# An S4 convolution and MLP mixer on one core: the spectra scratch laid out by frequency row, and a new order of the work

## The chip, the cores and the metric

The kernel runs on one core of one Trainium2 chip. The metric is device time in microseconds (us) of one execution; three executions of the kernel before took 552.21 to 555.27 us, with a median of 553.7. One more was profiled.

## The reference

All of it works on sequences of L = 2048 steps of D = 512 channels in float32. What matters here is the convolution, which is computed through spectra:

```python
xn = _layernorm(x, axis=-1)
# s = A(xn): a convolution over time, one filter per channel
P = jnp.exp(logdA[:, :, None] * l[None, None, :])
K = jnp.einsum("dn,dnl,dn->dl", Cc, P, dB).real          # (512, 2048)
Kf = rfft(pad(K, 2L));  Uf = rfft(pad(u.T, 2L))
y = irfft(Uf * Kf)[..., :L].T + u * Dskip
# g = silu(B(xn)): token shifts and an MLP
h = _gelu(_layernorm(x, axis=-1) @ w1)                    # 512 -> 512
x1 = x + concat(h's four quarters shifted by +1, -1, +2, -2) @ w2
x1 + _gelu(_layernorm(x1, axis=-1) @ w3) @ w4             # 512 -> 1376 -> 512
# the whole
return x + s * g
```

## The kernel before

**Tiling.** Time step t*16 + s lies in partition t of slice s of `X` [128, 16, 512], so the whole sequence stays in SBUF. The channels are worked on in two halves of DH = 256. A transform of the sequence is split in two steps over 64 rows of frequency ("g") with real and imaginary part ("e"), so 128 rows in all, and 16 slices with two parities ("s", "r").

**Stages.** `token_mixing` computes the layer norm, the first step of the input's transform (`u_stage1`, which stores `ue` to the DRAM scratch `scr_Ud`), and the shifted mixing. `tables` builds the filter in 16 chunks of 32 channels on ACT (exponentials, sines) and DVE (multiplies of the tile `wv`), sums over the states on PE, takes the first transform step of the filter on PE, and stores `k1e` to `scr_Kfa` (chunks 0 to 7) or `scr_Kfb` (8 to 15). `products` runs in 8 steps for each half: load `uin` and `kin` (rows of input and filter spectrum) and the constants `cst`; second transform step on PE (`spectrum`, into the PSUM banks `pc` and `pd`); complex product on DVE (`pr`, `kh`); first step of the inverse on PE; copies to `z1e` on ACT or DVE; a store to `scr_Zda` or `scr_Zdb`. `inverse` loads `zin`, takes the last step and multiplies it into `X`; `finish` adds the residual `xr` and stores the output. `mlp`, in eight groups of two slices, runs beside `tables` and `products`: its first matmuls write the banks `pb`, its second `pa`.

**Buffers.** Half 0 of `products` has one buffer for `uin` and `z1e` together (line 547: both rings begin at `early + K4`), one for `kin`, two for `cst`. Half 1 has three each of `uin`, `kin` and `z1e` and four of `cst` (lines 551 and 552); they lie where `tables` worked, so they come free when its last chunks are done.

**What sets the order.** Every operation is recorded by `Plan` with a number, in the order of the program's text. `ORDER` (lines 109 to 185) is a list of these numbers, with "a" for ACT or "v" for DVE where either can do the work. `Plan.issue` (line 313) emits the operations in that order to their engines; line 316 is where all of them are emitted, so the profile gives L316 for nearly everything, and tiles tell them apart. Each engine works through its own queue in order. Transfers are issued by SP, some of `X`, `xr` and the output by ACT. A DRAM scratch is tracked by its whole name: a load from `scr_Kfb` waits for all stores to it ahead of it.

**The scratch.** `scr_Ud` is [2 halves, 2, 16, 2, 64, 256], `scr_Kf` is [32, 2, 64, 256], `scr_Zd` is [16, 2, 2, 64, 256]. A row of 256 floats (1 KB) lies beside the rows of the neighbouring frequencies. `products` takes 4 frequencies from the lower half of g and 4 from the upper half at a step, so its loads and stores are in two halves (h = 0, 1), each with 64 partitions that move 4 KB in one run:

```python
g = h * NG // 2 + 4 * un
return dr[:, :, :, g : g + 4].rearrange("r s e g d -> (r s e) (g d)")
```

Of the kernel before, what the change touches and what calls it, by code (L numbers as in the profile page):

```python
# [10 lines left out]
F32 = mybir.dt.float32  # L11
# [13 lines left out]
S = 16  # L25
# [32 lines left out]
def shape_constants():  # L58
# [9 lines left out]
    first = np.stack([np.cos(a1), -np.sin(a1)], axis=1).reshape(NA, 2 * NG)  # L68
# [41 lines left out]
8 3 5 6 0 4 79 80 81 7 20 88 89 90 91 36 11 19 38 82 2 83 39 92 93 94 95 40 70 84 96a 85 78 31 86 22 87a 21 105 103 9  # L110
71a 106 104 107 596 10 97a 108 109 597 598 110 111 112 98 100v 101 599 122 13 23 123 113 114v 24 116v 117 99a 25 124
125 115a 601 602 119a 126 127 120 128 129 130 131 132 176 133 174 170 177 171 175 102a 134 172 26 138a 142 152 153a
173 178 179 137 180 181 15 139 157a 147 245 239 154a 241 246 143 182 183 184 243 135 240 242 158a 244 140a 118 141
186a 185a 189a 247 248 14 41 136 249 188a 16 190 17 42 205 121 250 43 45 44 46 144 148 149 192a 251 252 253 193 159
145a 150a 48 47 28 151 164 254a 167 155 51 200 156 50 207a 160 211a 257a 168 169 191 49 52 206a 195 196 146 27 53 310
194 201 208 210a 312 212 187a 202 209 230 255a 213 203a 161 204 225 226 197 217a 198a 199 165 166 54 218 30 55 214a
215 256a 29 235a 236a 313 238 237 232a 220 221 311 231a 162 227 228v 229 233 274 314 222 223a 163 308 315 309 316 224
396 397 317 234 280a 279a 609 276a 275a 299 216 258v 318 319 259 219 261v 320 262 18 281 282 269 56 321 57 59 64 37
304a 305a 277 322 270 278 325a 60 326v 61 62 324v 63 301a 32 58 72 300a 264 265 65 260 283a 284 343 263 66 68 271 67
294 323a 295 272v 307 306 348a 69 273 349a 631 286a 287 303 302 344a 345a 266 74 75a 267v 368 285 600 34 73a 76 268  # L120
603 398 296 297a 351 632 327v 350 374a 373a 77a 289 290 347 346 369a 370a 288 633 291 375 330v 292v 331 604 376 610
387 392v 328 399 400 401 371 293 606 332 402 403 404 405 372 389a 605 607 406 355v 608 388a 407 409 408 333 334 410
411v 413v 12 412 335 414 338 339 356 615 483 329 352v 298 340 426 482 611 487 618 499 484 498 336v 612 353 337 614
341v 390 503 485 363 358 504 613 488 428 391 33 364 424 486 359 425 505 489 342 365 500 357 616 637 354 382 383 429
430 434 427 432 617 360 377 501 619 620 640 378 366a 361a 384 479 621 622 367 431 393a 379 435 362 385a 386 653 491
433 448 449 654 380a 634 635 440 450 495 490 418 513 496 636 436 437 381 421 438 422 439 441 451 452 623a 655 656 657
423 492 419 493 442 420 517 443 638 453 512 514 539 446 454 518 447 455 515 502 519 35 525 456 494 639 543 497 659 642
516 520 641 561 565 444 445 460 461 662 462 415 658 463 529 464 465 624 625 521 476 626a 643 466 457 459 644 627a 628a
395 522 467 473 458 468 416 629a 477a 394 469 506 523 592a 474 472 547 524 470 645a 660 630 681 588a 589a 593a 675 676
590 538 507a 480a 646 677 678 508 680 535 478 661 647 540 664 648a 649a 663 684 665 666 509 679 682 650a 651a 705 697  # L130
526 594 667a 668 669 683 546 417 560 652 510a 481 511 706 685 595 591 798 686 536a 670a 548 687 688 707 532 799 708
709 533a 698 537 699 671a 562 805 800 806 554 555a 801a 710 701 534 812 700 702 703 556 813 802 551 807 827 828 819a
471 803 689a 704 820a 814 821 568 690 711 804 808a 809 810 557 558a 672a 673a 691 569a 712 829 811 822 559 574 815a
823a 570 713 816 824a 577 732 733 817 825 834 835 830a 831 716 715 674 734 818 575a 576 714 832 841 836 842 833 719
717 738 843a 718 692a 837a 838 693a 578a 826 848 849 855 721 720 735 850 856 694a 695a 741 862 571 722 572a 723 573
857 877 839 475 737 754 755 840 844 579 724a 845 756 736 725 757 739 726 863 846 878 869a 847 851a 852 696 858a 859
758 727a 728a 729a 730a 870a 740 743 742 530 871 759 864 853 854 860 861 879 872 865a 744 745 746a 884 760 776 777 885
891 873a 866 867 778 747 880a 874a 881 875 886 868 876 748 882 779 763 761 883 782 892 1299 762 780 893a 894 731 887a
1300 781 765 541 1301 1313a 749a 1292 750a 888 1293 1294 889 751a 764 890 766 767 752a 906 783 898 784 768a 552 899
895 1302a 1295a 785 908 1321 769 909 900 896 1296 549 1322 897 901 1314a 1303 903 904 753 910 935 1306 770 771a 772a  # L140
1307 1308 902 786 550 907 1315 905 1297 1298 1304 1305 787 788 789 1323 911 912 1309a 1316 527 1310 1328 1329 934
1317a 773a 1335 774a 913 1318a 1319 1324v 531 790a 1325 920 544 528 791 914 542 1330 1336 916 979 957 1311 1312 1331a
958 1326 915 917 1332 1320 959 775 1327 1337a 918 963 792 793a 1349 1350 919 1333 794a 1338 1334 1342 1343 922 921
1339 795a 796a 797 923 960 924 966 962 961 964 1344 1356 925a 926 927 936 1351 1352a 1003 1345a 1004 928a 1357 929a
930a 931a 1346 1005 1358 937 553 545 580 1340 933 938 940a 1341 965 939a 1006 1008 1371 1372 581 941 946 942 1007 1347
# [272 lines left out]
def kernel(  # L418
# [900 lines left out]
```

## Time and profile before

| | us |
|---|---|
| median of 3 runs (lowest to highest) | 553.7 (552.21 to 555.27) |
| the profiled execution | 549.68 |
| its span, first to last instruction | 547.9 |

Two more parts of the page, the slices and the queues:

```profile
PEclk9799899999989999999999999999998889989998
DMA  8999986556473622336529467676599999999968
...
q1 hardware_dynamic: 144544, 85.74, 68.6%
q10 hardware_dynamic: 4528, 4.46, 3.0%
...
HBM read 52.95 MB, written 29.36 MB: 150 GB/s over the span
```

A digit stands for a fortieth of the span, in tenths. `PEclk` is the granted clock of TensorE, `DMA` the mean busy share of the 16 DMA engines. `q1` holds SP's transfers, `q10` those of ACT: packets, MB, and the share of the engines' time. The two ends and the stretch from slice 30 on are where transfers fill the DMA engines.

### The profile page before, as it was taken

The numbers are of one execution on the slowest core, as the hardware profiler recorded it, in microseconds if no ns is written. First come the engines' busy times: TensorE is split into PE (matmuls) and PEld (weight loads), VectorE is DVE, ScalarE is ACT, GpSimd is POOL, SyncE is SP. The second block draws the span as 40 slices with busy tenths as digits, with TensorE's granted clock in tenths as the row PEclk, the third lists the DMA queues.
The fourth block names the chain that finished last, engine by engine and source line by source line (L and its number), as shares of the span: only waits on it lengthen the run. The fifth ranks groups of instructions, "written<-read, shape, count | busy, mean of one in ns | idle before, by whom it ended". The sixth has DMA issues, their size and how long they took to land.

```text
span 547.9 us, 14875 instructions
## 1 busy us (share of the span) xinstructions
PE 486.9 (89%) x6292; PEld 316.3 (58%) x6292; DVE 479.4 (88%) x772; ACT 415.1 (76%) x696; POOL 0.7 (0%) x6
## 2 busy tenths in 40 slices
PE   8796989997779999999999999897788798799982
PEld 7463655844448677666766656564554565366541
DVE  5999999999999999999999999999985578674575
ACT  4599899999899999999898999877732434337530
POOL 0000000000000000000000000000000000000000
PEclk9799899999989999999999999999998889989998
DMA  8999986556473622336529467676599999999968
GB/s 220 218 202 274 232 217 163 160 168 169 103 154 99 126 39 22 59 61 116 98 39 179 74 144 114 134 135 160 126 184 212 251 244 250 273 225 278 290 193 249
DMA packets 149138, 91.13 MB, mean 166 GB/s; under 512 B 103312, under 2 KB 136336, under 8 KB 148688
## 3 DMA queue, kind: packets, MB, share of 16 engines
q1 hardware_dynamic: 144544, 85.74, 68.6%
q10 hardware_dynamic: 4528, 4.46, 3.0%
q8 instruction: 49, 0.80, 0.6%
q14 instruction: 17, 0.14, 0.1%
HBM read 52.95 MB, written 29.36 MB: 150 GB/s over the span
## 4 chain that ended last, share of the span: by engine, by line
DVE 37%; PE 33%; DMA 11%; ACT 11%; issue 4%; SPq 2%; POOLq 0%; POOL 0%; ACTq 0%; DVEq 0%
DVE wv L316 15%; PE pa L316 12%; PE pb L316 11%; PE pc L316 6%; PE pd L316 4%; DVE X L316 4%; DVE stats L316 3%; ACT wv L316 2%; SPq L316 2%; DMA xr<-in_A_u_dram 2%; DVE up L316 2%; DVE ghl L316 2%; DMA uin<-scr_Ud 2%; DVE eg L316 2%; DMA scr_Zdb<-z1e 1%
## 5 line engine op out<-in xcount | busy, mean ns | idle before, releaser
L316 PE MATMUL pb<-x1T,w3h 128*128 128x256 f16 (+1 forms) x1056 | 124.3, 274 | 0.8 <-DMA x1T<-x1h 0.8
L316 PE MATMUL pa<-w4h,ghl 128*128 128x512 f16 (+1 forms) x528 | 123.0, 383 | 0.0
L316 PEld LDWEIGHTS <-w3h 128*128 128x128 f16 (+1 forms) x1056 | 102.6, 101 | 25.2 <-issue 10.5
L316 PEld LDWEIGHTS <-ghl 128*128 128x128 f16 (+1 forms) x528 | 50.0, 98 | 60.5 <-issue 8.3
L316 ACT ACT_TABLE_LOAD x50 | 64.2, 1283 | 10.0 <-DVE X L316 3.5
L316 ACT ACTIVATE wv<-wv 128x2080 f32<-128x2080 int32 x32 | 62.9, 1965 | 1.1 <-DVE wv L316 1.1
L316 ACT ACTIVATE ghl<-g,wsc 128x512 f16<-128x512 f32 (+1 forms) x37 | 25.0, 689 | 24.4 <-PE pa L316 22.5
L316 PE MATMUL pc<-wv 128*32 128x64 f32 x2048 | 34.3, 226 | 9.5 <-ACT z1e L316 4.2
L316 PE MATMUL pb<-xT,w1h 128*128 128x256 f16 x336 | 40.4, 283 | 0.7 <-ACT h L316 0.7
L316 ACT ACTIVATE g<-pb,wsc 128x512 f32<-128x512 f32 (+1 forms) x48 | 30.4, 650 | 13.8 <-PE pb L316 12.5
L316 PEld LDWEIGHTS pc<-wv 128*32 128x32 f32 x2048 | 31.4, 113 | 16.1 <-ACT z1e L316 8.2
L316 PEld LDWEIGHTS <-w1h 128*128 128x128 f16 x336 | 33.7, 101 | 9.1 <-issue 2.5
L316 DVE SCALAR_TENSOR_TENSOR ghl<-g,wsc,ghl 128x512 f16<-128x512 f32 (+1 forms) x48 | 33.5, 700 | 5.7 <-ACT ghl L316 5.5
L316 DVE TENSOR_TENSOR wv<-wv,eg 128x2048 f32<-128x2048 f32 x16 | 36.6, 2284 | 0.1
L316 DVE TENSOR_TENSOR wv<-mag,wv 128x2048 f32<-128x2048 f32 x16 | 36.5, 2284 | 0.0
L316 ACT ACTIVATE wv<-wv,halfpi 128x2080 f32<-128x2080 f32 x16 | 32.9, 2056 | 0.2
L316 ACT ACTIVATE mag<-par 128x128 f32<-128x128 f32 x132 | 32.5, 447 | 0.0
L316 PEld LDWEIGHTS <-hT 128*128 128x128 f16 x174 | 16.8, 99 | 21.4 <-issue 2.5
L316 DVE TENSOR_TENSOR pr<-pd,kh 128x512 f32<-128x512 f32 x32 | 20.7, 685 | 9.3 <-PE pd L316 8.1
L316 PE MATMUL pd<-uin,cst 64*32 64x256 f32 x512 | 20.9, 409 | 4.9 <-DMA uin<-scr_Ud 3.0
L316 DVE BATCH_NORM_STATS2 stats<-X 128x6 f32<-128x512 f32 x32 | 21.1, 683 | 4.2 <-DMA X<-in_A_u_dram 4.2
L316 PE MATMUL pc<-kev,kk 32*128 32x256 f32 x128 | 19.1, 417 | 5.8 <-DVE kev L316 5.7
(158 smaller groups left out, 854.2 us busy)
## 6 DMA issues: line engine op xcount, KB each, us to landing
wst<-in_B_w_dram SPq DMA_DIRECT2D x20, 512.0 KB, 4.3
scr_Ud<-ue SPq DMA_DIRECT2D x32, 256.0 KB, 2.8
uin<-scr_Ud SPq DMA_DIRECT2D x32, 256.0 KB, 4.8
scr_Kfa<-k1e SPq DMA_DIRECT2D x8, 512.0 KB, 5.2
cst<-c_gp SPq DMA_DIRECT2D x16, 256.0 KB, 4.6
kin<-scr_Kfa SPq DMA_DIRECT2D x16, 256.0 KB, 4.3
scr_Kfb<-k1e SPq DMA_DIRECT2D x8, 512.0 KB, 6.4
scr_Zda<-z1e SPq DMA_DIRECT2D x16, 256.0 KB, 3.6
```

The source lines that it names most:

```text
L316: ins = [getattr(self.engines[op.eng], name)(*args, **kw).ins for name, args, kw in op.calls]
```

## The change

The 128 rows (g and e together) become the outermost dimension of all three scratches, so that one row's data lie together, 32 KB for each half of the channels: `scr_Ud` is [2 halves, 128, 2, 16, 256], `scr_Kf` is [128, 2, 16, 256], `scr_Zd` is [128, 16, 2, 256]. The rows are put in a new sequence (`place`), by steps of `products`: step `un` takes rows 16 un to 16 un + 15. The constants `c_ks1`, `c_kk1`, `c_is2` and `c_gp` are permuted to match; their shapes stay. A load of `uin` or `kin` and a store of `z1e` is then one transfer of 128 partitions, in each 4 runs of 1 KB; a load of `zin` is one run of 4 KB in each of 128 partitions, where it was 4 of 1 KB. The stores of `ue` and `k1e` keep their runs (1 KB and 128 bytes).

```diff
+    place = np.arange(2 * NG).reshape(2, 2, NU, 4).transpose(2, 3, 1, 0).reshape(-1)
-    first = np.stack([np.cos(a1), -np.sin(a1)], axis=1).reshape(NA, 2 * NG)
+    first = np.stack([np.cos(a1), -np.sin(a1)], axis=1).reshape(NA, 2 * NG)[:, place]
...
 ORDER = """
-8 3 5 6 0 4 79 80 81 7 20 88 89 90 91 36 11 19 38 82 2 83 39 92 93 94 95 40 70 84 96a 85 78 31 86 22 87a 21 105 103 9
+5 0 8 7 3 88 89 6 79 80 81 82 90 91 92 93 83 2 94 95 22 21 105 84 85 9 106 86 103 96a 87a 97a 31 78 104 107 108 109
...
-    Ud = dram.tile([2, 2, S, 2, NG, DH], F32, name="scr_Ud")
+    Ud = dram.tile([2, P, 2, S, DH], F32, name="scr_Ud")
-    K1d = [dram.tile([NI, 2, NG, DH], F32, name=f"scr_Kf{h}") for h in "ab"]
-    Zd = [dram.tile([S, 2, 2, NG, DH], F32, name=f"scr_Zd{h}") for h in "ab"]
+    K1d = [dram.tile([P, 2, S, DH], F32, name=f"scr_Kf{h}") for h in "ab"]
+    Zd = [dram.tile([P, S, 2, DH], F32, name=f"scr_Zd{h}") for h in "ab"]
...
-        Q.dma_start(K1d[cc // 8][:, :, :, ch : ch + CQ].rearrange("i e g d -> (e g) i d"), k1e)
+        Q.dma_start(K1d[cc // 8][..., ch : ch + CQ].rearrange("p r s d -> p (r s) d"), k1e)
...
-    def by_g(dr, un, h):
-        g = h * NG // 2 + 4 * un
-        return dr[:, :, :, g : g + 4].rearrange("r s e g d -> (r s e) (g d)")
+    def by_g(dr, un):
+        return dr[16 * un : 16 * un + 16].rearrange("(c q) a b d -> (q a b) c d", c=4)
...
-            for t, dr in ((uin, Ud[hf]), (kin, Kd)):
-                for h in range(2):
-                    Q.dma_start(t[64 * h : 64 * h + 64].rearrange("p g d -> p (g d)"), by_g(dr, un, h))
+            for t, dr in ((uin, Ud[hf]), (kin, K1d[hf])):
+                Q.dma_start(t, by_g(dr, un))
...
-            for h in range(2):
-                Q.dma_start(by_g(Zd[hf], un, h), z1e[64 * h : 64 * h + 64].rearrange("p g d -> p (g d)"))
+            Q.dma_start(by_g(Zd[hf], un), z1e)
...
-        Q.dma_start(zin, Zd[hf][2 * g : 2 * g + 2].rearrange("s r e g d -> (e g) (s r) d"))
+        Q.dma_start(zin, Zd[hf][:, 2 * g : 2 * g + 2].rearrange("p s r d -> p (s r) d"))
...
-                    Ud[h, :, s + a].rearrange("r e g d -> (e g) r d"), ev_t[:, :, h * DH : (h + 1) * DH]
+                    Ud[h, :, :, s + a], ev_t[:, :, h * DH : (h + 1) * DH]
```

The whole of `ORDER` is new: 48 operations fewer, and every engine's queue is in another sequence from the start. Three places of it follow.

SP around the sixth step of half 0, before: `z1e_383` is that step's result, `uin_394` the next step's input, which takes the same buffer; `x1T` are transposes for the MLP; `k1e_392` is a late chunk of the filter.

```order
L316 DMA scr_Zda_63<-z1e_383 64x1024 x2
L316 DMA uin_394<-scr_Ud_60 64x1024 x2
L316 DMA_TRANSPOSE x1T_471<-x1h_473 128x8x128
L316 DMA_TRANSPOSE x1T_471<-x1h_475 128x8x128
L316 DMA kin_408<-scr_Kfa_61 64x1024
L316 DMA xr_588<-in_A_u_dram 64x4x256
L316 DMA kin_408<-scr_Kfa_61 64x1024
L316 DMA scr_Kfb_62<-k1e_392 128x32x32
```

And the same place now.

```order
L315 DMA scr_Zda_63<-z1e_383 128x4x256
L315 DMA xr_587<-in_A_u_dram 64x4x256
L315 DMA xr_588<-in_A_u_dram 64x4x256
L315 DMA uin_394<-scr_Ud_60 128x4x256
L315 DMA scr_Kfb_62<-k1e_392 4096x1x32
L315 DMA cst_406<-c_gp 128x512
L315 DMA kin_408<-scr_Kfa_61 128x4x256
```

Store and load are one row each, two loads of `xr` have moved between them, and the transposes have moved behind.

SP in half 1, before: `z1e_514` to `z1e_538` are results of the steps 0 to 3 of half 1 (514, 522, 530, 538), `uin_560`, `kin_553` and `kin_561` inputs of later steps.

```order
L316 DMA scr_Zdb_64<-z1e_530 64x1024
L316 DMA uin_560<-scr_Ud_60 64x1024
L316 DMA kin_553<-scr_Kfb_62 64x1024
L316 DMA scr_Zdb_64<-z1e_522 64x1024
L316 DMA cst_551<-c_gp 128x512
L316 DMA kin_561<-scr_Kfb_62 64x1024
L316 DMA is2_88<-c_is2 128x64
L316 DMA uin_560<-scr_Ud_60 64x1024
L316 DMA cst_559<-c_gp 128x512
L316 DMA zin_578<-scr_Zda_63 128x4x256
L316 DMA kin_569<-scr_Kfb_62 64x1024
L316 DMA scr_Zdb_64<-z1e_538 64x1024
```

And now, up to the store of `z1e_538`.

```order
L315 DMA cst_559<-c_gp 128x512
L315 DMA uin_552<-scr_Ud_60 128x4x256
L315 DMA scr_Zdb_64<-z1e_530 128x4x256
L315 DMA cst_567<-c_gp 128x512
L315 DMA_TRANSPOSE x1T_488<-x1h_492 128x8x128
L315 DMA zin_578<-scr_Zda_63 128x1024
L315 DMA kin_561<-scr_Kfb_62 128x4x256
L315 DMA scr_Zdb_64<-z1e_538 128x4x256
```

Before, the rows of 530 and 538 are one half each, with ten other issues between them; now each store is whole, and four issues stand between them.

ACT early in `token_mixing`, before, from the two scalings into `hT_117` (of the first slices) on; the activation of the next slices, into `h32_127`, comes five rows behind the last one shown.

```order
L316 ACTIVATE hT_117<-h32_118,wsc_76 128x2x256
L316 ACTIVATE hT_117<-h32_119,wsc_76 128x2x256
L316 ACTIVATE tm_106<-tm_106 128x512 x2
L316 ACTIVATE X_85<-X_85,bs_74,rs_71 128x512
L316 COPY ue_128<-pa1_92 128x512
L316 COPY ue_129<-pd1_98 128x512
```

And now, from the second of these scalings to that activation.

```order
L315 ACTIVATE hT_117<-h32_118,wsc_76 128x2x256
L315 COPY ue_129<-pd1_98 128x512
L315 COPY ue_129<-pd0_97 128x512
L315 ACT_TABLE_LOAD
L315 ACTIVATE rs_71<-mv_70,epst_67 128x8
L315 COPY ue_128<-pa1_92 128x512
L315 COPY ue_128<-pa0_91 128x512
L315 ACT_TABLE_LOAD
L315 ACTIVATE pn_105<-rawA_99 128x512
L315 ACT_TABLE_LOAD
L315 ACTIVATE h32_127<-pb0_93,wsc_76 128x512
```

The square root (`rs`), the arctangent (`pn`) and the Gelu (`h32`) alternate here, with three table loads in a place that had none. Over the whole program ACT has 54 table loads, where it had 50.

More of the change, by code (lines that the diff above doesn't have):

```diff
@@ new lines @@
+147 148 142 596 46 143 141 597 24 23 170 172 176 157a 174 177 173 604 205 47 149 175 171 155 48 49 178 50 144 160 51
+150a 145a 159 179 52 180 211a 210a 53 181 182 118 121 195 196 54 146 156 207a 206a 183 59 151 25 26 245 200 201 202 27
+184 185a 186a 243 189a 28 55 208 239 60 241 164 197 190 198v 230 192a 242 213 188a 56 246 187a 193 212 236a 209 240
+310 235a 232a 231a 274 191 308 244 214a 194 225 311 237 312 309 220 221 314 13 598 313 234 315 61 57 226 247 62 316
+248 317 249 233 203a 63 250 318 319 58 251 76 215 65 217a 606 238 280a 279a 64 252 320 204 253 218 66 68 29 255v 321
@@ new lines @@
+625 626a 643 627a 628a 644 489 645a 525 394 466 494 506 504 515 467 505 660 629a 468 675 516 469 676 502 507a 519 677
+477a 473 497 390 520 479 478 509 521 415 416 524 538 417 1 529 678 646 526 630 679 680 508 522 661 681 470 535 480a
+523 588a 589a 539 592a 682 546 593a 481 540 647 648a 649a 650a 543 561 663 664 684 665 536a 474 651a 705 697 590 532
+666 683 698 667a 668 533a 560 510a 547 591 594 707 708 595 669 710 565 798 799 819a 686 709 652 699 537 568 562 805
+670a 471 701 800 671a 672a 673a 806 807 700 702 511 685 687 703 472 688 801a 534 704 812 813 551 548 711 554 802 803
@@ new lines @@
+781 763 782 780 762 854 865a 866 860 879 783 898 861 867 872 886 874a 875 880a 876 749a 750a 751a 752a 891 892 899 868
+753 881 882 764 765 766 906 900 785 784 901 767 768a 887a 769 902 1275 1276 1268 903 904 893a 888 905 911 770 1269 908
+909 883 889 890 912 910 894 771a 772a 773a 1277 907 895 787 786 774a 1278a 1270 917 775 527 1289a 896 788 789 1271a
+913 790a 914 541 920 915 1272 1282 897 1290v 1297 1298 954 916 955 552 1283 1284 1273 1274 791 956 792 1291 793a 794a
+1299 1285a 1279 1293a 1280 1281 1300a 918 1292 795a 1304 796a 797 542 550 919 1286 544 921 1305 922 1294a 1295 1311
@@ new lines @@
+988 986 989 990 991 1336 1361 1343a 1344a 1008 993a 1007 1009 1010 1337 992a 995a 994a 1342 1356 1047 1062 1345 1350a
+1011a 1351 1362 996 1338 1091 1096 1357a 1019 1083 1012 1013 1049 1352 1014a 1015a 1016a 1017a 1084 1346 1368 1048
+1369 1088 1093 1085 1087 1092 1086 1050 1358 1021 1022 1375 1023a 1024a 1089 1020 1025 1353 1359 1360 1094 1095 1051
+1026 1090 1363a 1370 1376 1377 1030 1027 1031 1032 1028 1029 1033 1034 1035a 1036a 1097 1038a 1037a 1364 1365 1098
+1102 1378v 1118 1052 1099 1389v 1366 1053 1371a 1018 1382 1383 1367 1139 1054a 1101 1372 1055 1140 1056 1373 1105 1141
@@ new lines @@
+1100 1397 1057a 1058a 1059a 1060a 1379 1398 1064 1384 1065 1067a 1103 1145 1104 1066a 1390a 1391 1393a 1374 1385a 1386
+1039 1380 1063 1068 1404 1069 1073 1071 1394v 1070 1074 1381 1387 1388 1120 1072 1142 1144 1143 1075 1076 1395 1061
+1077 1079a 1078a 1107 1081a 1106 1392 1080a 1396 1405 1406 1108 1148 1109 1146 1110a 1111 1418 1182 1082 1119 1183
+1112 1407a 1399 1400a 1113a 1114a 1115a 1116a 1419 1147 1121 1411 1401 1184 1122a 1161 1123a 1163 1124 1129 1125 1412
+1130 1420 1432 1185 1187 1402 1403 1117 1126 1127 1131 1132 1128 1133 1135a 1137a 1150 1204 1134a 1433 1136a 1138 1162
@@ new lines @@
+1149 1413a 1151 1152 1408 1191 1186 1414 1188 1153a 1154 1225 1409 1425 1155 1434 1226 1189 1156a 1157a 1158a 1227
+1190 1426 1159a 1160 1427 1164 1206 1166a 1165a 1410 1421a 1167 1168 1172 1169 1170 1415 1171 1173 1228 1230 1447 1174
+1175 1193 1454 1176 1178a 1179a 1448 1192 1194 1177a 1180a 1229 1181 1195 1789 1428a 1196a 1422 1791 1416 1417 1423
+1231 1197 1234 1198 1199a 1200a 1201a 1202a 1429 1443a 1439a 1440a 1232 1424 1233 1207 1435a 1436 1430 1205 1209a 1431
+1441 1208a 1203 1210 1211 1792 1215 1213 1455 1247 1216 1212 1217 1218 1249 1214 1437 1438 1449 1236 1219 1222a 1461
@@ new lines @@
+1235 1442 1220a 1223a 1237 1238 1221a 1224 566 1444a 1445 1446 1239a 1560 1450v 1451 567 1240 1241 1456 1457v 1458
+1242a 1243a 1244a 1245a 563 564 1452 1250 1248 1468 1469 1246 1561 1462 1463v 1464 1252a 1251a 1731 1253 1258 1254
+1470 1453 1459 1259 1255 1460 1256 1257 1260 584 1261 1262 1265a 585 586 1475 1264a 587 1562 1263v 1563 1565v 1603
+1266a 1566 1571 1581 1564a 1465 1567 1582 1482 1483 1484 1572 1573 1574 1583 1568 1604 1267 1625 1569 1570 1575 1576v
+1577a 1623 1579v 1578v 1584 1587 1467 1586a 1602 1585v 1471a 1588 1476 1504 1592 1624 1589 1477 1593 1594 1497 1590
@@ new lines @@
+1591 1644 1595 1478v 1479 1596 1597v 1645 1598a 1605 1600a 1599v 1493v 1754 1608 1601 1606a 1472 1498 1667 1607a 1466
+1489a 1609 1473 1490a 1474 1646 1580 1613 1610 1611 1612 1614 1615 1616 1617 1485v 1486 1491 1492 1480 1621a 1665
+1619a 1620v 1741 1618a 1626 1627a 1628v 1499 1629 1687 1686 1481 1630 1500a 1634 1631 1632 1633 1635 1666 1487 1488
+1636 1637 1638 1639v 1501 1622 1707 1494a 1495 1640a 1738 1641a 1647 1642a 1650 1649a 1655 1648a 1651 1496 1745 1656
+1657 1652 1505 1511 1502 1653 1654 1790 1688 1643 1506 1658 1659 1660v 1661a 1512 1668 1663a 1662v 1507a 1671 1518
@@ new lines @@
+1670v 1676 1709 1503 1669a 1672 1677 1519 1520 1740 1673 1678 1708 1674 1679 1675 1680 1682a 1681v 1683v 1684a 1685
+1689 1691a 1690a 1508 1737 1692 1793 1697 1532 1739 1533 1732 1513a 1730 1693 1698 1525 1694 1695 1664 1696 1699 1700
+1701 1702v 1704v 1703v 1514 1728 1526 1710 1711v 1705a 1713 1794 1534 1714 1509 1510 1712a 1718 1715 1719 1546 1720
+1796 1706 1721 1795 1716 1717 1722 1724a 1515 1726v 1725a 1517 1742 1744 1723a 1746 1527 1727 1539 1540 1521a 1758
+1767 1522 1516 1523 1797 1747 1748 1759 1743 1528v 1749 1752 1751 1529 1541 1755 1757 1837 1756 1547 1733 1761 1524
@@ L185 @@
+1530 1760 1762 1771 1812 1531 1535v 1778 1536 1763 1764 1765 1768 1772 1553 1735 1774 1773 1542v 1537 1753 1543 1729
+1766 1538 1548 1549v 1550 1544 1545 1554 1555v 1734 1769 1801 1770 1782 1775 1551 1552 1556 1808 1557 1559 1779 1558
[3 rows of a table added]
 """
```

100 lines of the change are left out of this document (25 added, 75 removed), and 6 rows, old and new, of the table ORDER.

## The prediction

> **What bounds the kernel now.** I read the page first (busy time by engine, then the slices), then busy time by stage in windows that I cut at events of the timeline, then the chain of waits and PE's waits in the stage where the engines are not full.
>
> ```profile
> span 547.9 us, 14875 instructions
> PE 486.9 (89%) x6292; PEld 316.3 (58%) x6292; DVE 479.4 (88%) x772; ACT 415.1 (76%) x696; POOL 0.7 (0%) x6
> 0.00:55.00 55.00, 42.11 (x257) 31.78 (x259) 46.80 (x132) 40.99 (x69) 0.70 (x6) 0.94 0.99 228
> 55.00:405.50 350.50, 327.73 (x4484) 213.72 (x4492) 343.34 (x462) 319.81 (x546) 0.00 (x0) 0.98 0.59 126
> 405.50:425.40 19.90, 15.58 (x301) 8.53 (x286) 10.58 (x26) 7.19 (x17) 0.00 (x0) 0.91 0.92 196
> 425.40:495.80 70.40, 61.70 (x984) 39.59 (x984) 49.23 (x99) 26.78 (x45) 0.00 (x0) 0.93 1.00 248
> 495.80:526.00 30.20, 29.69 (x203) 17.61 (x200) 14.89 (x27) 19.26 (x22) 0.00 (x0) 1.00 0.98 287
> 526.00:547.90 21.90, 10.13 (x81) 5.07 (x80) 14.59 (x28) 1.06 (x1) 0.00 (x0) 0.91 0.68 207
> ```
>
> After a window's length come the busy times of PE, weight loads, DVE, ACT and POOL, then PE's granted clock, the DMA engines' busy share and GB/s. No engine is full over the whole span, but each stage has its own limit. To 405.5 it is DVE: 343.34 of 350.5 us after the head, with ACT at 319.81. From 425.4 to 495.8 it is none of the engines alone: PE works 61.70 of 70.4 us at a clock of 0.93, while the DMA engines are busy all the time (1.00). From 495.8 to 526 it is PE, 29.69 of 30.2. The cuts are these events:
>
> ```profile
> 404.31 1.22 DVE L316 SCALAR_TENSOR_TENSOR wv<-up,wv 128x1024 f32<-128x1024 f32 x1
> 425.35 1.25 PE L316 MATMUL pd<-uin,cst 64*32 64x256 f32 x32 [0.58 <-DVE z1e L316]
> ...
> 495.79 0.04 PE pd L316 x4
> ...
> 520.84 5.20 PE pa L316 x24
> ```
>
> The first is the last multiply of the last of 16 `tables` chunks; the second the first spectrum of `products` for half 1; the third the last matmul of `products`' inverse; the fourth ends the last MLP matmul. I call the stages A (to 405.5), B (19.9), C (70.4), D (30.2) and E (21.9). The same events bound them in the changed kernel, where C opens with the other spectrum of the same step.
>
> **Part 1: fewer, wider transfers.** Loads of `uin` and `kin` and stores of `z1e`, 96 transfers of 64 partitions, become 48 of 128. Each carries 512 KB in runs of 1 KB, where a half carried 256 KB in runs of 4 KB; `zin` goes from runs of 1 KB to 4 KB.
>
> ```profile
> wst<-in_B_w_dram SPq DMA_DIRECT2D x20, 512.0 KB, 4.3
> scr_Ud<-ue SPq DMA_DIRECT2D x32, 256.0 KB, 2.8
> uin<-scr_Ud SPq DMA_DIRECT2D x32, 256.0 KB, 4.8
> kin<-scr_Kfa SPq DMA_DIRECT2D x16, 256.0 KB, 4.3
> scr_Zda<-z1e SPq DMA_DIRECT2D x16, 256.0 KB, 3.6
> kin<-scr_Kfb SPq DMA_DIRECT2D x16, 256.0 KB, 6.9
> zin<-scr_Zdb SPq DMA_DIRECT2D x8, 512.0 KB, 7.0
> ...
> L316 SPq DMA_DIRECT2D uin<-scr_Ud x32: 444/562/4705, 233.3 to 473.6; - x32
> ```
>
> An issue holds SP 0.56 us (the median), so two halves are complete 0.56 + 4.8 = 5.4 us after the first issue. The trace has no 512 KB load of these tensors. Bounds: 4.3 us, which the 128-partition `wst` loads of the same size need in runs of 1 to 2 KB, and 7.0, which `zin` needs in runs of 1 KB in the saturated end. I take 4.3 to 5.4, near `wst`, because the half-0 steps run where the DMA engines are 0.59 busy. A step's load then changes by -1.1 to +1.6 us, its store by -0.6 (one issue) to about the same loss.
>
> In half 0 every step waits for its own round trip, since `z1e` and `uin` share one buffer: store, landing, load, spectrum. The waits in part 2 show PE idle 2.4 us for it once, in the last of the eight steps. Forty-eight issues fewer free SP of 48 x 0.56 = 27 us. That is nothing except where SP is a burst long:
>
> ```profile
> 407.62 3.65 DMA scr_Zda<-z1e
> ...
> 411.84 4.88 DMA uin<-scr_Ud
> ...
> 428.74 7.05 DMA cst<-c_gp
> ...
> 459.23 0.54 SPq L316
> ...
> 466.17 0.45 SPq L316
> ...
> 467.07 8.10 DMA scr_Zdb<-z1e
> 475.20 4.09 DMA xr<-in_A_u_dram
> ```
>
> Between the two SP rows stand eight more issues, one directly behind another, 7.4 us in all, and at their end half of a `z1e` store (its other half stands nine places later in the queue). Its landing 8.10 us later, and `xr` behind it, hold a buffer and so PE. In the new SP order the two halves are one store.
>
> **Part 2: stage C.** These are PE's waits from 405 to 496:
>
> ```profile
> PE pc L316 <- ACT z1e L316: 4.9, 5, 3.0
> PE pc L316 <- DMA cst<-c_gp: 2.9, 1, 2.9
> PE pd L316 <- DMA uin<-scr_Ud: 2.4, 1, 2.4
> ...
> PE pc L316 <- DMA xr<-in_A_u_dram: 0.7, 1, 0.7
> ```
>
> The 3.0 is the wait of the chain above; the others on `z1e`, 0.4 to 0.6 each, are PSUM evacuations and stay. So 3.0 + 2.9 + 0.7 = 6.6 us of idle PE in C comes from late transfers. A clock of 0.93 over 70.4 us costs 4.9 us more; D, which has hardly any idle time, runs at 1.00.
>
> The new PE order has three groups of twelve `pb` matmuls more in C and one group of six `pa` matmuls fewer; D has the reverse. From
>
> ```profile
> 483.03 2.73 PE pb L316 x24
> ```
>
> and the `pa` x24 above, that is 3 x 2.73/2 - 5.20/4 = +2.8 us: C has 61.7 + 2.8 = 64.5 us of PE work, D 30.2 - 2.8 = 27.4. If all late transfers and the slow clock go: 64.5 - 4.9 + 2.1 = 61.7. If none goes: 64.5 + 8.7 = 73.2. C moves 70.4 x 248 = 17.5 MB; at D's 287 GB/s, reached with `zin` and `xr` in runs of 1 KB, this takes 60.8 us, at 248 it takes 70.4. I take the middle rate, 267: 65.4, and round up to **66**.
>
> B is a round trip (last `k1e` store, then `kin` of half 1): two issues instead of three, and fewer ahead of them: **19.0**, bounds 17 to 21. E has the same operations with one `out` store earlier: **21.9**.
>
> The Trainium skill speaks against the small runs: page "DMA: Bandwidth & Descriptors", section "Why small descriptors are slow (HBM only)", counts about 3 cycles for each packet beside one for every 32 bytes. By this a run of 1 KB costs 35 cycles and one of 4 KB 131, so four small runs cost 7% more (an estimate from that page). If two thirds of C's traffic paid that, C would be some 3 us longer. The trace's densest traffic in small runs, the 287 GB/s of D, shows no such loss beside 248.
>
> **Part 3: the new order in A.** The work on DVE ahead of the last multiply is the same but for swaps with ACT. Over the kernel four `X` scalings more go to DVE and three `z1e` copies fewer:
>
> ```profile
> L316 ACT ACT_TABLE_LOAD x50 | 64.2, 1283 | 10.0 <-DVE X L316 3.5 <-PE pb L316 3.4 <-issue 2.3
> L316 DVE TENSOR_SCALAR X<-X,rs,bs 128x512 f32<-128x512 f32 x3 | 1.6, 545 | 0.0
> L316 DVE COPY z1e<-pd 128x256 f32<-128x256 f32 x11 | 4.2, 417 | 3.0 <-PE pd L316 3.0
> ```
>
> 4 x 0.545 - 3 x 0.417 = +0.9 us; the other swaps nearly cancel. ACT gets 54 table loads for 50; up to the last multiply there are nine more, 9 x 1.283 = 11.5 us, and behind it five fewer. ACT idles 30.7 us between 55 and 405.5, and 14 in the head, so most of this is covered. If none were, A would grow by 11.5. I take +2: A = **407.5**. It can't fall far, because DVE's idle time there is 15.3 us in all, 8.2 of it in the head, where it waits for inputs.
>
> Edits at nothing: the permuted constants (same shapes), and the stores of `ue` and `k1e`, whose runs stay 1 KB and 128 bytes but now lie far apart. Their landing (2.8 us for `ue`) hides behind 200 us of work. Without that cover only the last `k1e` store, in B, would count.
>
> **Sum.** 407.5 + 19.0 + 66 + 27.4 + 21.9 = 541.8, against 547.9. The execution took 1.8 us beyond its span (549.68), so 543.6. The median of the runs, 553.7, stands 0.73% above the profiled execution; times 553.7/549.68 this is **547.5 us**, 1.1% faster.
>
> **Rivals.**
> 1. *The late transfers stay.* The DMA engines are full in C with either layout, and SP waits for landings, not for issues. For it: the share of 1.00, and 1 KB runs that are no larger than before. Then C = 73.2, B = 19.9, the sum 549.9: +0.4%, median 555.7, no change.
> 2. *The half-0 round trip gets longer (slower).* Place: the wait of `uin`'s spectrum behind `z1e`'s store in A, where DVE's queue is in order and its next multiply waits for that spectrum. Price: a load at `zin`'s 7.0 instead of 5.4 is 1.6 us late in each of seven steps, 11 us. It decides as soon as a load of 512 KB lands later than 5.4 us. Two issues of `xr` (which wait for a PE group) also stand between store and load of one step in the new SP queue. Late loads would help C no more either: 407.5 + 11 + 19.9 + 73.2 + 27.4 + 21.9 = 560.9, median 566.8. Against it: 7.0 was measured where the engines are full; here they are 0.59 busy.
> 3. *The pitch hurts.* `ue` and `k1e` now store, and `zin` now loads, at a pitch of 32 KB from partition to partition. If this halved `zin`'s rate, its 16 x 512 KB = 8.4 MB, at 287 GB/s 29 us, would take 58, and of the 29 more some 20 would show at the end: about 562 of span, median 568. Against it: the present `uin` halves read at a pitch of 64 KB and land in 4.8 us. The Trainium skill, page "DMA: Bandwidth & Descriptors", section "Latency and other measured facts", warns of row pitches at large powers of two, with its rates from 512 KiB up; no run here shows it.
> 4. *All waits go.* C = 61.7, B = 17, A = 405.5: 533.5, median 539.2.
>
> **How the numbers follow.** Forecast 0.50, rival 1 0.20, rival 2 0.17, rival 3 0.04, rival 4 0.09. A measurement of this kernel can tell about 0.5% from no change. The forecast's own spread (A by 4, C by 4) reaches into "same" with a tenth of its chance, so faster 0.54, same 0.25, slower 0.21. The range of 538 to 563 takes in the forecast, rival 1, most of rival 4, and that part of rival 2 in which C still gains (541.8 + 11 = 552.8, median 558.7).
>
> **What would show it.** Right: the last table multiply ends within 404 to 411; from the first half-1 spectrum to the last inverse takes 62 to 69 us, with the DMA rate above 255 GB/s and the clock above 0.95; `uin` lands in under 5.4 us at 512 KB. Wrong: `uin` at 6 to 7 us with DVE waiting for PE `pd` before 400 (rival 2); PE's waits on `cst` or `z1e` of 2.5 us and more still there (rival 1); a last stretch above 25 us with `zin` landing above 10 (rival 3); or an ACT so full that DVE waits for it before 405, which would break part 3.

## The result, and the profile after

The changed kernel takes 536.57 us in the median (536.13 to 539.68, 4 runs), the kernel before 553.22 beside it (552.21 to 555.27): a ratio of 0.971, with a 95% interval of 0.966 to 0.975. That is faster by 2.9%, where 1.1% was forecast, and 1.4 us below the low end of the range. The profiled execution took 536.33 us.

The busy times of the whole page, and windows as before (lengths, then PE, weight loads, DVE, ACT, POOL, PE's clock, share and rate of the DMA engines). They are cut at the same events, except that the cut at 406.2 lies 1.1 us ahead of the end of the last table multiply:

```profile
span 534.5 us, 14802 instructions
PE 486.1 (91%) x6292; PEld 311.9 (58%) x6292; DVE 476.8 (89%) x773; ACT 417.1 (78%) x699; POOL 0.7 (0%) x6
```

```profile
0.00:55.00 55.00, 43.07 (x234) 31.10 (x235) 46.09 (x132) 44.59 (x84) 0.70 (x6) 0.81 0.84 212
55.00:406.20 351.20, 329.44 (x4489) 212.10 (x4487) 341.44 (x466) 322.40 (x534) 0.00 (x0) 0.98 0.57 130
406.20:424.10 17.90, 16.97 (x313) 10.77 (x310) 11.38 (x25) 12.17 (x23) 0.00 (x0) 1.00 0.93 203
424.10:487.80 63.70, 59.70 (x1016) 38.08 (x1016) 47.84 (x96) 24.97 (x44) 0.00 (x0) 1.00 0.98 277
487.80:515.20 27.40, 27.12 (x171) 14.75 (x172) 15.74 (x29) 11.89 (x15) 0.00 (x0) 1.00 0.92 301
515.20:534.50 19.30, 9.83 (x80) 5.10 (x80) 14.30 (x28) 1.06 (x1) 0.00 (x0) 0.90 0.76 227
```

No engine works noticeably less (PE 486.1 us for 486.9, DVE 476.8 for 479.4), and the mean clock over the span is 0.965 in both: it is lower in the first 55 us now (0.81 for 0.94) and higher in B and C. So the 13.4 us are idle time and, in B and C, slow clock. In C the clock is 1.00 and the DMA engines move 277 GB/s at a share of 0.98, where they moved 248 at 1.00. The last table multiply ends at 407.3 by the timeline (`wv`, 406.07 + 1.22), so A is 407.3 and B 16.8:

```profile
406.07 1.22 DVE L315 TENSOR_TENSOR wv<-up,wv 128x1024 f32<-128x1024 f32 x1
```

```profile
407.30:424.10 16.80, 15.87 (x303) 9.81 (x301) 10.28 (x24) 11.07 (x19) 0.00 (x0) 1.00 0.96 209
```

| stage, us | before | forecast | after |
|---|---|---|---|
| A | 405.5 | 407.5 | 407.3 |
| B | 19.9 | 19.0 | 16.8 |
| C | 70.4 | 66 | 63.7 |
| D | 30.2 | 27.4 | 27.4 |
| E | 21.9 | 21.9 | 19.3 |
| span | 547.9 | 541.8 | 534.5 |

All of PE's waits from 405 to 490, after (total, times, longest):

```profile
PE pc L315 <- DVE z1e L315: 2.5, 5, 0.5
PE pb L315 <- DMA x1T<-x1h: 1.3, 1, 1.3
PE pc L315 <- DVE kev L315: 0.9, 1, 0.9
PE pc L315 <- ACT z1e L315: 0.2, 1, 0.2
```

The waits of 3.0, 2.9 and 2.4 us on `z1e`, `cst` and `uin` are gone; none is longer than 1.3. And the transfers, with their size and their median time from issue to landing:

```profile
uin<-scr_Ud SPq DMA_DIRECT2D x16, 512.0 KB, 5.2
...
zin<-scr_Zdb SPq DMA_DIRECT2D x8, 512.0 KB, 9.4
```

A whole `uin` lands in 5.2 us, twice the bytes in the time of a half (4.8).

### The profile page after: what moved, and what is told of

Same layout as the page of the kernel before. It is cut to its first block, busy times and chain, and to the rows that moved or that the text cites. A ratio compares the mean times of both kernels' runs of the same rounds, so it can differ in the third digit from the quotient of the medians.

```text
span 534.5 us, 14802 instructions
## 1 busy us (share of the span) xinstructions
PE 486.1 (91%) x6292; PEld 311.9 (58%) x6292; DVE 476.8 (89%) x773; ACT 417.1 (78%) x699; POOL 0.7 (0%) x6
## 4 chain that ended last, share of the span: by engine, by line
PE 42%; DVE 27%; ACT 18%; DMA 8%; issue 5%; SPq 0%; ACTq 0%; DVEq 0%
PE pb L315 14%; PE pa L315 14%; DVE wv L315 11%; PE pc L315 8%; ACT wv L315 7%; PE pd L315 5%; DVE X L315 4%; DMA x1T<-x1h 2%; ACT L315 2%; DVE ghl L315 2%; ACT ue L315 1%; DVE pr L315 1%; DMA zin<-scr_Zda 1%; DMA scr_Ud<-ue 1%; ACT wst L315 1%
## 5 line engine op out<-in xcount | busy, mean ns | idle before, releaser
L315 DVE TENSOR_TENSOR wv<-par,ev 128x1056 int32<-128x1056 f32 x16 | 20.0, 1248 | 5.7 <-PE pc L315 5.7
L315 PE MATMUL pb<-w2h,hT 128*128 128x512 f16 x87 | 21.1, 395 | 2.6 <-DVE X L315 2.6
```

The costliest lines, as they stand in the source:

```text
L315: ins = [getattr(self.engines[op.eng], name)(*args, **kw).ins for name, args, kw in op.calls]
```

## The experiments

Twelve experiments were run, each beside the kernel before. All times are us. "Queue" is the time of the packets of the main DMA queue (`q1`, SP's transfers, 85.7 MB in every kernel) for each of the 16 engines: its share of the span times the span. Packets can overlap (some stretches below have a share above 1), so it tells how long packets take, not how long an engine can do nothing else. B and C are given together, because in some traces the matmul records that mark the cut between them are missing.

| kernel | median | ratio to before, 95% interval | A | B + C | D | E | queue |
|---|---|---|---|---|---|---|---|
| before (first profile) | 553.2 | | 405.5 | 90.3 | 30.2 | 21.9 | 376 |
| e8 before again | 554.6 (one) | | 409.1 | 91.8 | 30.2 | 21.7 | 374 |
| e5 old order, halves side by side | 551.9 | 0.997 (0.993 to 1.001) | 410.7 | 87.1 | 30.2 | 21.9 | 372 |
| e1 old order, whole transfers | 540.2 | 0.976 (0.971 to 0.981) | 409.6 | 77.5 | 30.2 | 21.6 | 349 |
| e7 e1, one out store moved | 539.9 | 0.975 (0.971 to 0.980) | 407.7 | 78.3 | 30.2 | 21.6 | 347 |
| e12 e1, six out stores moved | 537.5 | 0.971 (0.967 to 0.976) | 406.7 | 78.2 | 30.2 | 20.2 | 348 |
| e2 new order, old layout, halves | 541.3 | 0.979 (0.974 to 0.984) | 407.0 | 83.4 | 28.0 | 19.4 | 370 |
| e3 new order, new layout, halves | 543.9 | 0.984 (0.977 to 0.990) | 411.7 | 84.9 | 27.2 | 19.4 | 370 |
| e10 after, halves in half 0 | 541.4 | 0.978 (0.973 to 0.982) | 409.8 | 81.9 | 27.1 | 19.4 | 358 |
| e11 after, halves in half 1 | 539.8 | 0.977 (0.973 to 0.980) | 407.2 | 83.9 | 27.5 | 19.4 | 357 |
| e9 after, two wide transfers | 536.2 | 0.969 (0.964 to 0.973) | 410.5 | 79.5 | 26.9 | 19.4 | 345 |
| after | 536.6 | 0.971 (0.966 to 0.975) | 407.3 | 80.5 | 27.4 | 19.3 | 344 |
| e6 after, one out store last | 537.0 (one) | | 407.2 | 80.7 | 27.1 | 20.2 | 345 |

**e1 and e2: each part of the change alone.** e1 takes the changed kernel with the order of before:

```diff
+    def empty(self):
+        self.new().alts = {"SP": [0.0, []]}
...
                 Q.dma_start(t, by_g(dr, un))
+                plan.empty()
...
```

> New layout and single transfers of 128 partitions, but every engine's order is that of the kernel before (the place of each second half in the SP queue is left empty). Theory 'transfers' (the wide single transfers free stage C, the new order only fits the program to them): 538 to 543 us, C 62 to 66 us (it was 70.4), PE's waits on cst and uin gone from C. Rival 'order' (the order written anew does it): 551 to 555 us, C 69 to 73, the 3 us waits on z1e and cst still there. Half of each would be 544 to 549.

e2 takes the kernel before with the order of the changed one, each pair at the place of the single transfer:

```diff
+                with plan.together():
                     for h in range(2):
                         Q.dma_start(t[64 * h : 64 * h + 64].rearrange("p g d -> p (g d)"), by_g(dr, un, h))
...
```

> Layout and half transfers of the kernel before (runs of 4 KB, 64 partitions), but the order of the changed kernel, the two halves of each load or store one behind the other at the place of the single one. Theory 'transfers': 548 to 556 us, because two issues stand where one stood and a half transfer uses half of the SBUF side; C above 68 us, B near 19 or 20. Rival 'order': 536 to 540 us, C 63 to 65, B below 18.

Measured: 540.2 and 541.3, so either part alone brings most of the gain, 13 and 12 us of 16.6. For e1 the theory held and the rival fell. For e2 the time lies between the two, 1.3 us above the rival's range and 6.7 below the theory's. The two parts largely replace each other. C of e1:

```profile
409.60:487.10 77.50, 70.63 (x1260) 43.69 (x1260) 59.59 (x124) 33.34 (x59) 0.00 (x0) 1.00 1.00 280
```

```profile
PE pc L322 <- ACT z1e L322: 2.8, 6, 0.6
PE pc L322 <- DVE z1e L322: 1.7, 3, 0.7
PE pd L322 <- DMA uin<-scr_Ud: 1.3, 1, 1.3
```

With no word of the order changed, B and C take 77.5 us together for 90.3, the rate is 280 GB/s, the long waits are gone and the clock is 1.00. In e2, with halves, the same stretch has

```profile
407.00:490.40 83.40, 76.89 (x1317) 49.70 (x1316) 58.23 (x121) 36.15 (x64) 0.00 (x0) 1.00 1.04 254
```

The engines stay full at 254 GB/s. The new order doesn't make the packets faster (370 us of queue time, for 372 with halves side by side in the old order, e5); its PE waits are short (the longest in C is 1.2) and the clock stays up. By its profile e2 saves 6.9 us in B + C, 2.2 in D and 2.5 in E.

**e3 and e4: what in the transfers does it.** e3 is the changed kernel with each transfer split by partitions, in the new layout; e4 the old layout with both halves in one transfer whose outer dimension is 2:

```diff
-                Q.dma_start(t, by_g(dr, un))
+                with plan.together():
+                    for h in range(2):
+                        Q.dma_start(t[64 * h : 64 * h + 64], by_g(dr, un)[64 * h : 64 * h + 64])
...
```

> The changed kernel, with each load of uin and kin and each store of z1e split into two transfers of 64 partitions, one behind the other; layout (runs of 1 KB) and order stay. If it is the width and number of the transfers that counts: 544 to 552 us, equal to the run with old layout and new order within 2 us. If the layout in DRAM itself counts (what lies in one row, not how many transfers): 536 to 539, and the old layout with the new order is slower than this. If the order does it all: 536 to 539 for both.

```diff
+    def by_g2(dr, un):
+        halves = dr.rearrange("r s e (h g) d -> h (r s e) g d", h=2)
+        return halves[:, :, 4 * un : 4 * un + 4]
...
+                Q.dma_start(t, by_g2(dr, un))
...
```

> Layout of the kernel before and order of the changed kernel, with both halves of a row in one transfer (two blocks of 64 partitions, 4 KB each, in one descriptor list). If one issue in place of two is what counts: 536 to 540 us, uin landing in 5 us or less. If the transfer's shape counts (a list whose outer dimension is 2 is dealt to few of the 16 DMA engines): uin landing above 10 us and the whole above 560. No difference from the halves in the new order would say that neither counts.

Measured: e3 543.9, 7 us slower than the changed kernel, and 2.6 above e2 (541.3), where at most 2 were expected; their intervals overlap, and the queue time is 370 us in both, though e3's halves go in runs of 1 KB and e2's in runs of 4 KB. So the layout by itself brings nothing. e4 took 892.8 us (ratio 1.61). From 280 us on, where its products run, its window shows (the last two columns are share and rate of the DMA engines)

```profile
280.00:892.00 612.00, 289.95 (x3680) 165.98 (x3680) 215.33 (x336) 164.15 (x270) 0.00 (x0) 0.72 0.39 84
```

and of PE's waits from 400 to 500

```profile
PE pd L314 <- DMA uin<-scr_Ud: 47.6, 3, 17.9
```

The rate is 84 GB/s at a share of 0.39, and one load is waited for 17.9 us. So one issue is no gain if the transfer's shape is bad, and this is what the new layout is for: it gives a row of 128 partitions one stride. The Trainium skill, page "DMA: Bandwidth & Descriptors", section "Why a DMA increments its semaphore by 16 and not by 1", says that the number of engines is the largest one up to 16 that divides the slowest dimension on both sides, which here gives 2. The low share agrees; no view here shows single engines.

**e5: place in the queue, or width.** The kernel before, with the second half of each transfer directly behind the first:

```diff
...
-            for h in range(2):
-                Q.dma_start(by_g(Zd[hf], un, h), z1e[64 * h : 64 * h + 64].rearrange("p g d -> p (g d)"))
+            with plan.together():
+                for h in range(2):
+                    Q.dma_start(by_g(Zd[hf], un, h), z1e[64 * h : 64 * h + 64].rearrange("p g d -> p (g d)"))
+            plan.empty()
```

> The kernel before with its layout, its half transfers and its order, except that the second half of each uin, kin and z1e transfer stands directly behind the first half in SP's queue (before, the second halves stood up to nine places later). Theory 'place' (what the single transfer bought in stage C is that a row's second half no longer stands late in the queue): 540 to 546 us, B + C 77 to 83 us (90.2 before, 77.5 with whole transfers in the old order), no wait of PE of 2.5 us and more on z1e, cst or uin. Rival 'width' (fewer issues and 128 partitions at once are needed): 549 to 555 us, B + C 86 to 91.

Measured: 551.9, a ratio whose interval holds 1, in the rival's range. B and C shrink to 87.1, of which 77.5 was to be had, so the place is a quarter of it, and a third if the 91.8 of e8 below is taken for the kernel before. The prediction's own picture of the gain (half of a `z1e` store nine places late) is a part of it at most; whether the rest is the width or the number of transfers, e9 tells.

**e9: width, or number of transfers.** The changed kernel with two transfers for one, cut across columns:

```diff
-                Q.dma_start(t, by_g(dr, un))
+                with plan.together():
+                    for h in (0, 2):
+                        Q.dma_start(t[:, h : h + 2], by_g(dr, un)[:, h : h + 2])
...
```

> The changed kernel with every uin, kin and z1e transfer again made of two, one behind the other, but cut across the columns: each has all 128 partitions and half of the bytes, in the same runs of 1 KB. As many transfers and issues as with two halves of 64 partitions (543.9 us). Theory 'width' (a transfer to 64 partitions keeps the DMA engines busy longer for the same bytes): 536 to 539.5 us, the main queue's busy time 64 to 65.5% of the span as in the changed kernel (68.2% with halves), B + C 80 to 82.5 us. Rival 'number' (two issues and two latencies where one stood): 542 to 545 us, B + C 83.5 to 86.

Measured: 536.2, as fast as the changed kernel. The main queue of e3 (first) and of e9, with packets, MB and share:

```profile
q1 hardware_dynamic: 156832, 85.74, 68.2%
```

```profile
q1 hardware_dynamic: 156832, 85.74, 64.3%
```

The same packets and bytes, cut into as many transfers: 0.682 x 543.2 = 370 us of packet time for each engine when they go to 64 partitions, 0.643 x 536.3 = 345 when they go to 128. Forty-eight issues more cost nothing. The 96 transfers carry 25.2 MB, 1536 runs of 1 KB for each engine, so a run took 26/1536 us = 17 ns longer on average. The Trainium skill, page "DMA: Bandwidth & Descriptors", section "Rules for kernel authors", says of two transfers to disjoint partition halves that they serialize and that one of 128 partitions should be used. The advice agrees; the reason that the runs show is the time of the packets, not that there are two transfers.

**e10 and e11: where it counts.** Halves only in half 0 (e10, shown here), or only in half 1 (e11, with `hf == 1`). In both the store of `z1e` is split in the same way:

```diff
+                if hf == 0:
+                    with plan.together():
+                        for h in range(2):
+                            Q.dma_start(t[64 * h : 64 * h + 64], by_g(dr, un)[64 * h : 64 * h + 64])
+                else:
+                    Q.dma_start(t, by_g(dr, un))
...
```

> The changed kernel with two transfers of 64 partitions instead of one only in the products of half 0 (stages A and the start of B). Theory (the DMA engines have room in A, but z1e's store and the next uin load lie in a round trip that the table multiplies wait for; this is what made A 411.7 with halves everywhere): A 409.5 to 412, B + C 80 to 82, the whole 539 to 542 us. Rival (with the engines 0.6 busy nothing is felt, and the 4.4 us more of A were spread from run to run): A 406.5 to 408, the whole 536 to 538.

> The changed kernel with two transfers of 64 partitions instead of one only in the products of half 1 (stage C and the end of B), where the DMA engines are full. Theory: A 406.5 to 408, B + C 83.5 to 86 us at 250 GB/s instead of 80.5 at 263, the whole 539.5 to 542 us. Rival (in C other work hides it): B + C 80 to 82, the whole 536 to 538.

Measured: 541.4 and 539.8; beside e9 on the same chip their intervals lie wholly above its own. Both places cost, 5.2 and 3.6 us over e9, and the sum is near the 7.7 by which e3 lies over e9. The queue's time splits too: 358 and 357, between 344 and 370. e11's stretch and e9's:

```profile
407.20:491.10 83.90, 76.92 (x1316) 49.59 (x1316) 58.15 (x120) 36.07 (x63) 0.00 (x0) 1.00 1.08 252
```

```profile
410.50:490.00 79.50, 75.83 (x1316) 47.75 (x1315) 58.18 (x121) 36.06 (x63) 0.00 (x0) 1.00 0.98 267
```

In half 1 the engines are full, so longer packets lengthen the stretch: of its 4.4 us more, 2.6 are one wait of PE for a late `x1T`. In half 0 they aren't full; there the row of DVE's waits from 300 to 405 in e10 is

```profile
DVE pr L315 <- PE pd L315: 5.8, 4, 4.1
```

where the changed kernel has 0.5 us in all: the round trip of store and load, felt once. But the profiles don't place the 5.2 us there: A is 409.8 in e10 and was 410.5 in e9, without such a wait, and e10's profiled execution is only 1.9 us longer than e9's. That halves in half 0 cost is shown by the medians, the way they do it is not.

**e6, e7 and e12: stage E.** e6 moves one ACT store of `out` to the end of the changed order, where the old order has it; e7 moves it from there in e1:

```diff
 ORDER (e6)
-1805 1787 1813 1814 1815 1806 1809 1810 1811 1807 1824 1816 1818 1825 ... 1835 1836
+1805 1787 1813 1814 1815 1806 1809 1810 1811 1807 1824 1816 1825 ... 1835 1836 1818
```

> The changed kernel with one edit: the ACT store of out for half 1, rows 3, is the last thing that ACT issues, as in the kernel before, instead of directly behind its sum. If stage E shrank because no out store is left over behind the last sums: E 20.0 to 20.9 us instead of 19.3, the last issue 0.6 to 1.3 us later. If E shrank for another reason (the sums on DVE themselves, 14.9 us now and 15.6 before): E stays at 19.3 to 19.6.

```diff
 ORDER (e7)
-1864 1868 ... 1890 1891 1866
+1864 1866 1868 ... 1890 1891
```

> The first run (whole transfers, old order) with one edit: the same ACT store of out moves from the end of ACT's queue to its place behind its sum. If the leftover store is what made E long: E 20.0 to 20.7 us instead of 21.6, the whole 538.5 to 540. The other out stores that stand in a late bunch there keep E above 19.3. If the bunch alone matters: E 21.3 to 21.9, the whole 540 to 541.

Measured: E of 20.2 in e6 as expected, but 21.6 in e7, no better than e1; the one store isn't the cause there. ACT's issues of `out` in the tails of e7 and of the changed kernel (ns, least, median, most):

```profile
L322 ACTq DMA_DIRECT2D out_dram<-X x8: 653/1372/1551, 523.8 to 533.5; - x8
```

```profile
L315 ACTq DMA_DIRECT2D out_dram<-X x6: 630/635/637, 519.8 to 530.2; - x6
```

In the old order stores that have been ready for long stand behind one that waits for its sum; they leave in a bunch from 523.8 on, and an issue takes 1.37 us in the median, for 0.64. e12 moves five of these ahead, and the last one too:

```diff
 ORDER (e12)
-1799 1855 1812 1854 ... 1864 1868 1835 1811 ... 1865 1836 ... 1866
+1799 1836 1812 1825 1855 1811 1835 1854 ... 1864 1866 1868 ...
```

> The first run (whole transfers, old order; E 21.6 us, 540.2 us) with the out stores of the tail no longer bunched: the three ACT stores and two SP stores of half 0 that stood behind half 1's first stores (which wait for their sum) go ahead of them, and the store at the end of ACT's queue goes behind its sum. Theory (E is long in the old order because in-order queues hold finished stores back until 10 us before the end, where each issue then takes 1.2 to 1.5 us instead of 0.6): E 19.2 to 20.2 us, no issue of out above 1 us in the last 8 us, the whole 537 to 539. Rival (E is long because of the order of the sums on DVE): E 21.2 to 21.8, the whole 539.5 to 541.

Measured: E of 20.2, at the end of what was expected, and 537.5 us; no issue of `out` in the last 8 us takes more than 0.69. The last sums on DVE, in e12 and in the changed kernel:

```profile
530.07 0.69 DVE L248 TENSOR_TENSOR X<-X,xr 128x512 f32<-128x512 f32 x1
```

```profile
529.46 0.69 DVE L315 TENSOR_TENSOR X<-X,xr 128x512 f32<-128x512 f32 x1
```

and, from the timeline of the kernel before, ACT's nine issues and the last sum:

```profile
527.51 16.54 ACTq L316 DMA_DIRECT2D out_dram<-X  x9
...
541.01 0.69 DVE L316 TENSOR_TENSOR X<-X,xr 128x512 f32<-128x512 f32 x1
```

The last sum stands 535.3 - 530.76 = 4.5 us before the end in e12, 534.5 - 530.15 = 4.4 in the changed kernel, and stood 547.9 - 541.70 = 6.2 before it. So 1.8 us of the 2.6 lie behind the last sum, where the late stores stood. The rest is in the sums: from the end of D to the last of them it is 15.0 us in the new order and 15.7 in the old.

**e8: the kernel before, profiled again.**

> The kernel before, unchanged, profiled a second time. If the first profiled execution (549.7 us) was a quick one of a kernel that mostly takes 552 to 555, this one should take 552 to 555, and the stage in which it is longer shows what varies. If profiling itself makes the execution shorter, it takes 549 to 550.5 again.

Measured: 554.6, of which A 409.1 and B + C 91.8. The first profiled execution was a quick one. The waits in B and C cost 1.5 us more this time, and the clock shows how a wait goes on costing:

```profile
475.00:480.00 5.00, 5.00 (x50) 2.14 (x50) 4.00 (x8) 2.64 (x3) 0.00 (x0) 1.00 1.06 250
480.00:485.00 5.00, 0.65 (x22) 0.61 (x24) 0.76 (x2) 0.65 (x2) 0.00 (x0) 0.97 1.25 280
485.00:490.00 5.00, 5.00 (x80) 4.00 (x65) 2.55 (x5) 0.58 (x1) 0.00 (x0) 0.69 0.97 260
```

PE idles for most of 5 us, and the 5 us after it run at 0.69. The first profile has the same around 435, where by its timeline a spectrum waits 2.95 us for `cst`,

```profile
435.92 2.08 PE L316 MATMUL pc<-kin,cst 64*32 64x256 f32 x32 [2.95 <-DMA cst<-c_gp]
```

and the clock in the window behind it is 0.50:

```profile
435.00:440.00 5.00, 4.08 (x66) 2.89 (x67) 0.86 (x2) 0.59 (x1) 0.00 (x0) 0.50 1.13 167
```

A wait doesn't always do this. In e11 PE waits 2.59 us at 467 for `x1T`, and the 5 us behind it run at 1.00. The changed kernel and e6, which has the same order up to its last operations, both wait 2.6 us at 152; each wait stands with the 2.5 us behind it, the changed kernel first:

```profile
155.13 1.35 PE L315 MATMUL pb<-w2h,hT 128*128 128x512 f16 x3 [2.56 <-DVE X L315]
...
155.10:157.60 2.50, 2.47 (x7) 0.90 (x7) 2.46 (x3) 2.47 (x4) 0.00 (x0) 0.53 0.65 196
```

```profile
155.25 1.02 PE L315 MATMUL pb<-w2h,hT 128*128 128x512 f16 x4 [2.55 <-DVE X L315]
...
155.20:157.70 2.50, 2.45 (x12) 1.07 (x11) 2.46 (x3) 2.47 (x4) 0.00 (x0) 1.00 0.64 201
```

So the slow clock behind a wait comes in one execution and not in another, and no run here shows what decides it.

## Why the prediction was right in direction and too small

- **Four terms were too long.** Of the 10.9 us between 547.5 and 536.57, 4.0 are the scaling to the median, 2.6 E, 2.3 C and 2.2 B; A and D are within 0.2. The direction, and that the waits and the slow clock of C would go, was right; these four sizes were not, and the reason given in part 1 was mostly another than the runs show.
- **C, 2.3 us too long: the middle was the wrong choice.** The step that failed is "I take the middle rate, 267": the rate came to 277, and C to 63.7 for 66. All of the 4.9 us of slow clock came back: PE is busy for 59.70 us, and the prediction's own 64.5 - 4.9 is 59.6. What lies above its end "all go" (61.7) is idle time, 4.0 us for the 2.1 that it left. It priced 6.6 us of waits and 4.9 of clock as two things; in C of the kernel before the slow clock stands behind the long waits (0.50 behind the 2.95 us), so they went together.
- **The reason for the rate was wrong.** Part 1 counted issues (0.56 us each, 27 us on SP) and the place of the second half. e9 keeps all 96 issues and loses nothing; e5 puts the halves side by side and gains at most 0.7%. What counts with whole transfers is that a run of bytes takes longer when its transfer covers 64 partitions (370 us of queue time for 345). The rows of before held halves only, and the step compared run lengths, which e2 against e3 show to matter little (370 us for both).
- **The landing.** `uin` was taken at 4.3 to 5.4 us; it is 5.2. The gain isn't a quicker landing but more bytes in the same time.
- **B, 2.2 us too long: the wrong path.** The step took B as "a round trip (last `k1e` store, then `kin` of half 1)" and priced issues. In the profile of before the chain through B is another: the last `z1e` store of half 0 (3.65 us) and the `uin` load behind it (4.88), for which PE waits 2.4 us, and a clock of 0.91, worth another 1.8 us of the 19.9. The prediction had that wait in part 1 and didn't count it here. In the changed kernel PE has no wait above 0.9 us in B and a clock of 1.00. e1 has neither the long wait nor the slow clock and takes 16.0 us; e5 with halves has a wait of 1.7 on `uin`, a clock of 0.92, and 20.1 us.
- **E, 2.6 us too long.** "Same operations with one `out` store earlier" read the list of operations, not the queue: in the profile of before ACT's nine issues of `out` are spread over 16.5 us, the last of them behind the last sum. e12 gives 1.4 of it back by the place of six stores.
- **A and D were right.** A +1.8 for +2 of forecast, though A alone moves between 405.5 and 411.7 from kernel to kernel, so this proves little. D came out at 27.4 as worked out from the moved matmuls.
- **Scaling to the median, 4.0 us, the largest.** "Times 553.7/549.68" (which gives 547.6) carried the 0.73% of a quick execution over to the new kernel. e8 has 3.6 us of the excess in A, which scatters in both kernels, and 1.5 in B and C with their waits, which the change removes; the changed kernel's profile is at its median (536.33 and 536.57).
- **The rivals.** Late transfers stay: no, by PE's waits. A longer round trip in half 0: no with whole transfers (DVE waits 0.5 us), though e10 shows the place to be real. The pitch of 32 KB: `zin` of half 1 lands later, in 9.4 us for 7.0, but D ran at 301 GB/s and in the 27.4 us forecast. All waits go: nearly this, with 534.5 us of span for 533.5, but in part by luck: A and C are 1.8 and 2.0 us longer than it says, and E, which it left at 21.9, is 2.6 shorter.

The new order wasn't needed for the gain: e12, with the old one but for six out stores, is within 0.9 us of the changed kernel, and the intervals overlap. What stays open is which of its moves saves 12 us when the transfers are halves (e2); its waits in C are short, but A's share of it can't be told from A's scatter. Nor did any run show why a transfer to 64 partitions is slower. The loads of `xr` and the stores of `out` are halves as well. Partition 64 r + t of `X` holds time step (2 t + r) * 16 + s (not t * 16 + s, as said under "Tiling"), so its 128 partitions have no single stride in DRAM, and e4 shows the price of merging such halves; another layout of X wasn't tried.

## What to carry to other kernels

Where the DMA engines are full, price a transfer by the time that its packets take (the queue's share times the span), not by its issues: here 128 partitions with one stride in DRAM took 345 us where twice 64 took 370. A wait of PE of 2 to 3 us can cost a spell of slow clock beside its length, so look at the clock behind the waits before you take the middle between "all waits go" and "none". Follow the chain through each stage before you price it: B's went by another transfer than the one that was priced. And before scaling a forecast by the distance of a profile from the median, ask whether the stages that vary are those the change removes.

## What the hardware showed beside this

- Runs of 1 KB were no dearer than runs of 4 KB in half transfers: 370 us of queue time with both. In e3 25.2 MB of halves go in runs of 1 KB and the 8.4 MB of `zin` in runs of 4 KB; in e2 it is the reverse.
- The same wait of 2.6 us was followed by a clock of 0.53 in one execution and of 1.00 in another (the changed kernel and e6, at 152 us).
- An issue of `out` on ACT takes 0.64 us where the stores are spread (the changed kernel) and 1.37 in the bunch of e7, so a late bunch of stores is slow in its issues too.
- A profiled execution of the same kernel took 549.7 us once and 554.6 another time, 0.9% apart.
